# A decode layer with its backward pass on one core: the chain between the two halves reordered, side products one step later

## The chip, the cores and the metric

The kernel runs on one core of a Trainium2 chip. The metric is the device time of one execution in microseconds (us). Before the change it took 1754.85 us in the median of four runs (1751.91 to 1758.08).

## The reference, cut to what matters

```python
def _fwd_reference(A_x, A_k_cache, A_v_cache, A_wq, A_wo, B_x, B_w1, B_w3, B_w2):
    def _A_ref(x, k_cache, v_cache, wq, wo):          # B=4, H=32 heads, Sk=4096, Dh=128, D=512
        q = (x @ wq).reshape(B, Sq, H, Dh).transpose(0, 2, 1, 3)
        scores = jnp.einsum("bhqd,bhkd->bhqk", q, k_cache) * (Dh ** -0.5)
        p = _softmax(scores, axis=-1)
        o = jnp.einsum("bhqk,bhkd->bhqd", p, v_cache)
        return o.transpose(0, 2, 1, 3).reshape(B, Sq, H * Dh) @ wo
    def _B_ref(x, w1, w3, w2):                        # F=1792
        h = _silu(x @ w1) * (x @ w3)
        return h @ w2
    h = x + _A_ref(_layernorm(x), A_k_cache, A_v_cache, A_wq, A_wo)
    return h + _B_ref(_layernorm(h), B_w1, B_w3, B_w2)

_out, _vjp = jax.vjp(_f, A_x, A_k_cache, A_v_cache, A_wq, A_wo, B_w1, B_w3, B_w2)
return (_out, *_vjp(grad_out))
```

One token for each of four batch entries attends to a cache of 4096 keys and values in 32 heads, and the gradients of everything are returned. K and V are 134 MB each, and so are their gradients, so some 700 MB pass through the DMA engines.

## The kernel before, in words

The order of all instructions is written out by hand; nothing reorders them. SBUF holds 22 equal slots of about 1 MB (class `Slot`). A slot is taken from the front of the list `free` and put at its back by `give()` while the program is being written. On the chip, a load into a slot waits until the last reader or writer of the slot's former content is done. All loads are issued by one in-order queue, SP's; all large stores by GpSimd's (POOL's). So a load that waits for its slot holds up every load behind it.

**Forward half** (until about 674 us). For each of the 128 pairs of batch entry and head, K and V are loaded. `M_mm(s)` multiplies V with `PK`, the keys weighted by the probabilities, on TensorE (PE, line 436). `M_end(s)` ends that pair and gives two slots back. `kP_flush` (lines 457 to 461) turns a sum of 32 pairs round. The last pairs are 125, 126 and 127.

**The chain in the middle.** Eight loads are queued behind the last V: the two halves each of w1 and w3 (line 543), then four pages of wo of eight heads each (line 549). Transposed copies w1T and w3T are made by `w13T` (16 units, 112 transposes of 128x128 on PE at line 566; `evac_copy` at lines 216 and 218 takes each unit out of PSUM on ScalarE, ACT, or VectorE, DVE). `attn_page(pg)` multiplies the attention output with one page of wo (line 481), and DVE adds the partial sums to the residual rows `hrows` (line 487). `woT` transposes wo in place, 16 units of 8 transposes (line 575). Then come the second layernorm (`layernorm_rows`, lines 232 to 238), the transposes of its rows (line 768), the products with w1 and w3 (`gu_ps`, line 780), the element-wise work of the gate (lines 799 to 809), the products with w3T and w1T (`dn_ps`, line 817), the layernorm's gradient (lines 827 to 844), the products with the transposed wo (`dOT_ps`, line 848) and what follows from them (lines 852 to 867).

While the chain runs, w1, w3, w1T, w3T, the wo pages and eight slots of `M` fill 20 of the 22 slots. Loads of V for the backward half (`load_V2`, line 749) can use only the rest, until `gu_ps` has read w1 and w3 and `dn_ps` has read w1T and w3T.

**Backward half.** For each pair `s`, `front(s)` transposes V (`V_T`: PE line 739, ACT line 740) and forms `dP_ps` (line 1046). `back(s)` writes the gradient of V as one product on DVE (`gv`, line 1053), scales dP (lines 1068 and 1071), writes the gradient of K (`gk`, line 1053), and stores both (lines 1065 and 1075). In the loop, `front(s + 1)` precedes `back(s)`. `prefetch` lets loads of V run seven pairs ahead. After each `back(s)`, one or more steps of `side_work` are taken: a generator that forms all the other gradients in small pieces, each with one product on PE and one copy on ACT (`grad_unit`, lines 881 and 882).

Of the kernel before, what the change touches and what calls it, by code (L numbers as in the profile page):

```python
# [9 lines left out]
FP32 = mybir.dt.float32  # L10
# [14 lines left out]
def kernel(  # L25
# [448 lines left out]
    def attn_page(pg):  # L474
        last = pg == H // 8 - 1
        if pg == 0 or last:
            hold["at"] = psX.tile([P, 512], FP32, tag="x", name="at_ps")
        at_ps = hold["at"]
        for k in range(8):
            c = 0 if last else k % 4  # L480
            nc.tensor.matmul(at_ps[32 * c:32 * c + B, :], lhsT=OT_bf[:, (8 * pg + k) * B:(8 * pg + k + 1) * B],
                             rhs=wo_page(8 * pg)[:, k].rearrange("p c n -> p (c n)"),
                             start=(k == 0 if last else pg == 0 and k < 4), stop=(k == 7 if last else pg == H // 8 - 2 and k >= 4),
                             tile_position=(0, 32 * c))
        if pg >= H // 8 - 2:
            for c in range(1 if last else 4):
                nc.vector.tensor_tensor(out=hrows[:], in0=hrows[:], in1=at_ps[32 * c:32 * c + B, :], op=ALU.add)
# [90 lines left out]
    pending = deque()  # L578
    for nm, ap in (("w1", B_w1), ("w3", B_w3)):
        for i in range(2):  # L580
            pending.append((load_w13_half, nm, ap, i))
# [111 lines left out]
    weights(NGI)  # L693
    w13T(4, "sv")
    M_mm(NH - 2, 0, SJ)
    M_end(NH - 2)
    weights(NGI)
    w13T(4, "sv")
    M_mm(NH - 1, 0, SJ)
    M_end(NH - 1)  # L700
    weights(NGI)
    O_cols(NH - MC, NH)
    w13T(len(tunits), "sv")
    kP_flush(NH - 1)
    for pg in range(H // 8 - 1):
        attn_page(pg)
        woT(4, "sv")
    attn_page(H // 8 - 1)
# [43 lines left out]
    with ExitStack() as cm:  # L752
# [3 lines left out]
        psT = cm.enter_context(tc.tile_pool(name="psTm2", bufs=4, space=bass.MemoryType.PSUM))  # L756
        hs = Slot("hhat")
        hhat = hs.f(D)[0:B, :]
        while free:
            load_V2()  # L760
        layernorm_rows(hrows[:], B, hhat, rstd_h[:])
        nc.scalar.activation(out=warm[:], in_=warm[:], func=AF.Exp)
        woT(len(wo_units), "s")
        hhatT = mid.tile([P, DC, B], BF16, name="hhatT")
        hhatT_f = mid.tile([P, DC, B], FP32, name="hhatT_f")
        pt = psA.tile([P, DC, B], FP32, tag="rT", name="pt_hT")
        for c in range(DC):
            nc.tensor.transpose(pt[:, c, :], hhat[:, c * P:(c + 1) * P], ident_f[0:B, 0:B])
        nc.vector.tensor_copy(out=hhatT[:], in_=pt[:])
        nc.vector.tensor_copy(out=hhatT_f[:], in_=pt[:])  # L770
        nc.gpsimd.tensor_copy(out=hhat_bf[:], in_=hhat)
        hs.give()
        while free:
            load_V2()
        w1, w3 = mid_w["w1"], mid_w["w3"]
# [6 lines left out]
        for sl in w1 + w3:  # L782
            sl.give()
        while len(free) > 1:
            load_V2()

        rdiag = mid.tile([B, B], FP32, name="rdiag")
        nc.vector.tensor_scalar(out=rdiag[:], in0=ident_f[0:B, 0:B], scalar1=rstd_h[:], scalar2=None, op0=ALU.mult)
        rb_ps = psA.tile([P, B], FP32, tag="rT", name="rb_ps")
        nc.tensor.matmul(rb_ps[:], lhsT=ones_f[0:B, :], rhs=rdiag[:], start=True, stop=True)  # L790
        rb = mid.tile([P, B], FP32, name="rb")
        nc.vector.tensor_copy(out=rb[:], in_=rb_ps[:])
        gateT = mid.tile([P, FC, B], FP32, name="gateT")
# [15 lines left out]
        nc.vector.tensor_tensor(out=hhT_bf[:], in0=siluT[:], in1=gu_ps[:, 1], op=ALU.mult)  # L809
        V_T(0, psT)  # L810

# [8 lines left out]
        for sl in mid_w["w1T"] + mid_w["w3T"]:  # L820
            sl.give()
        while len(free) > 1:
            load_V2()
        V_T(1, psT)

# [15 lines left out]
                                       in1=u[:], op0=ALU.mult, op1=ALU.add)  # L841
        nc.vector.tensor_tensor(out=u[:], in0=u[:], in1=rb[:, None, :].to_broadcast([P, DC, B]), op=ALU.mult)
        nc.vector.tensor_tensor(out=dhT[:], in0=u[:], in1=grT[:], op=ALU.add)
# [26 lines left out]
    with ExitStack() as c2:  # L870
# [5 lines left out]
        bw3 = c2.enter_context(tc.tile_pool(name="bw3", bufs=3, reuse_waits="tile"))  # L876

        def grad_unit(dst, lhsT, rhs):
            n = rhs.shape[-1]
            ps = psg.tile([P, 512], FP32, tag="gps", name="gps")  # L880
            nc.tensor.matmul(ps[:, 0:n], lhsT=lhsT, rhs=rhs, start=True, stop=True)
            nc.scalar.copy(out=dst, in_=ps[:, 0:n])

        def side_work():
            dq_ps = psx.tile([P, 512], FP32, tag="x2", name="dq_ps")
            for s in range(NH):
                nc.tensor.matmul(dq_ps[:, s:s + 1], lhsT=M_of(s)[:, 0:Dh], rhs=dOT_f[:, s:s + 1], start=True, stop=True)
                if s % MC == MC - 1:
                    Ms[s // MC].give()
                if s % 3 == 2:  # L890
                    yield
            t = rs.f(2080)[:, 1536:1536 + NH]
            nc.vector.tensor_tensor(out=t, in0=c_rep[:], in1=kPT[:], op=ALU.mult)
# [4 lines left out]
            nc.scalar.copy(out=dqr_bf[:], in_=pt[:])  # L898
            flat = Slot("dqflat")
            for b in range(B):  # L900
                nc.sync.dma_start(out=flat.b(HD)[b:b + 1, :], in_=dqr_bf[b::B, :])
# [15 lines left out]
            for ch in range(H // HH):  # L917
# [6 lines left out]
                for hl in range(0, HH, 2):  # L924
                    pt = psg.tile([P, 2, DC, P], BF16, tag="gps", name="pt_wq")
                    for i in range(2):
                        for cc in range(DC):
                            nc.tensor.transpose(pt[:, i, cc, :], wv[:, cc, (hl + i) * Dh:(hl + i + 1) * Dh], ident_b[:])
                    nc.scalar.copy(out=wqT.b(HH * D).rearrange("p (n c) -> p n c", c=P)[:, hl * DC:(hl + 2) * DC, :],
                                   in_=pt.rearrange("p a c k -> p (a c) k"))  # L930
                    yield
                wq2.give()
                for hl in range(HH):
                    h = ch * HH + hl
                    nc.tensor.matmul(dx_ps[0:B, :], lhsT=dqT_bf[:, h * B:(h + 1) * B], rhs=wqT.b(HH * D)[:, hl * D:(hl + 1) * D],
                                     start=(h == 0), stop=(h == H - 1))
                yield
            wqT.give()
            fs = Slot("fin")
            dxhat, lnbx = fs.f(2 * D)[0:B, 0:D], fs.f(2 * D)[0:B, D:2 * D]  # L940
# [8 lines left out]
            for cc in range(DC):  # L949
                st = Slot("gwq")  # L950
                for n8 in range(HD // 512):
                    grad_unit(st.b(HD)[:, n8 * 512:(n8 + 1) * 512], xhat_bf[0:B, cc * P:(cc + 1) * P],
                              flat.b(HD)[0:B, n8 * 512:(n8 + 1) * 512])
                    yield
                nc.gpsimd.dma_start(out=out_4[cc * P:(cc + 1) * P, :], in_=st.b(HD))
                st.give()
# [5 lines left out]
            for sl in w2:  # L962
                sl.give()
            h2_bf = rs.t[0:B, 2560:2560 + D]
            nc.vector.tensor_tensor(out=h2_bf, in0=hrows[:], in1=o2_ps[0:B, :], op=ALU.add)
# [4 lines left out]
            for dst_rows, srcT in ((hh_rows, hhT_bf), (dg_rows, d_gateT_bf), (du_rows, d_upT_bf)):  # L970
                for c0 in range(0, FC, 7):
                    pt = psg.tile([B, 7, P], BF16, tag="gps", name="pt_Tr")
                    for c in range(7):
                        nc.tensor.transpose(pt[:, c, :], srcT[:, c0 + c, :], ident_b[:])
                    nc.scalar.copy(out=dst_rows[:, c0 * P:(c0 + 7) * P].rearrange("b (c f) -> b c f", f=P), in_=pt[:])
                    yield
            for i in range(2):
                st = Slot("gw2")
                for k in range(7):
                    fc = 7 * i + k  # L980
                    grad_unit(st.b(7 * D)[:, k * D:(k + 1) * D], hh_rows[:, fc * P:(fc + 1) * P], gr_bf[0:B, :])
                    yield
                nc.gpsimd.dma_start(out=out_8[i * 7 * P:(i + 1) * 7 * P, :].rearrange("(c p) j -> p c j", p=P),
                                  in_=st.b(7 * D).rearrange("p (c j) -> p c j", c=7))
                st.give()
            for (rows, out_ap) in ((dg_rows, out_6), (du_rows, out_7)):
                for i in range(2):
                    st = Slot("gw13")
                    for k in range(2):
                        for (f0_, w_) in f_chunks:  # L990
                            grad_unit(st.b(2 * F)[:, k * F + f0_:k * F + f0_ + w_],
                                      hhat_bf[0:B, (2 * i + k) * P:(2 * i + k + 1) * P], rows[:, f0_:f0_ + w_])
                            yield
                    nc.gpsimd.dma_start(out=out_ap[i * 2 * P:(i + 1) * 2 * P, :].rearrange("(c p) f -> p c f", p=P),
                                      in_=st.b(2 * F).rearrange("p (c f) -> p c f", c=2))
# [11 lines left out]
            for h0 in range(0, H, 8):  # L1007
                st = Slot("gwo")
                for k in range(8):
                    h = h0 + k  # L1010
                    grad_unit(st.b(8 * D)[:, k * D:(k + 1) * D], oflat.b(HD)[0:B, h * P:(h + 1) * P], dh_bf[0:B, :])
                    yield
                nc.gpsimd.dma_start(out=out_5[h0 * P:(h0 + 8) * P, :].rearrange("(h p) j -> p h j", p=P),
                                  in_=st.b(8 * D).rearrange("p (h j) -> p h j", h=8))
# [69 lines left out]
        for s in range(NH):  # L1084
# [5 lines left out]
            back(s)  # L1090
            step("s", 1 if s < 42 else 2 + s % 2)
        step("s", 400)
# [30 lines left out]
```

## Time and profile before

| | |
|---|---|
| median of four runs | 1754.85 us |
| profiled execution: time / span of its instructions | 1749.55 us / 1747.8 us |
| moved by DMA | 707.86 MB, mean 405 GB/s |
| busy: PE, DVE, ACT, POOL | 76%, 72%, 55%, 28% of the span |
| mean granted TensorE clock | 0.729 of full speed |

The page cuts the span into 40 slices of 43.7 us and gives the busy share of each in tenths. The view by stretches gives, for stretches that one chooses, the busy time of each engine with its count of instructions, the granted clock, the DMA share (the mean busy share of the 16 DMA engines) and what they moved. The view of waits says who waited for whom. The timeline lists instructions with the idle time ahead of them in brackets.

### The profile page before, as it was taken

The page shows a single profiled execution, that of the slowest core. Times are in us where ns is not written, and L with a number is a line of the kernel's source. Part 1 is how long each engine was busy: PE and PEld are TensorE (multiplying, and loading weights), DVE is VectorE, ACT ScalarE, POOL GpSimd, SP SyncE. Part 2 cuts the span into 40 slices and gives each one's busy share as a digit, 9 for nine tenths or more (in the row PEclk, how much of TensorE's full clock was granted, in tenths as well). Part 3 has the DMA queues.
Part 4 walks back from the last instruction along what each step waited for, and adds up shares of the span by engine and source line. Part 5 has one row for each costly group of instructions (what it writes and reads, how often), then busy time and mean ns, then how long its engine had stood idle before and what let it go on. Part 6 is the DMA issues. An engine that isn't in the chain of part 4 may idle for free.

```text
span 1747.8 us, 44078 instructions
## 1 busy us (share of the span) xinstructions
PE 1331.9 (76%) x18993; PEld 1127.6 (65%) x18993; DVE 1254.0 (72%) x1385; ACT 954.3 (55%) x1460; POOL 488.9 (28%) x805
## 2 busy tenths in 40 slices
PE   5889888788888887888877876777776778485573
PEld 4667666677666666778777875555565556365463
DVE  5899899889898995557856757566464667475585
ACT  3455445445444544555554655576666667475463
POOL 2333333333333330112421333222222223132132
PEclk8999999999999999655555556675555555556555
DMA  9999999999999998699999999999999999999997
GB/s 398 410 418 418 419 418 419 419 414 418 417 414 399 418 405 302 261 420 421 415 420 421 417 418 414 423 379 426 422 416 420 415 406 411 420 402 413 424 417 290
DMA packets 107123, 707.86 MB, mean 405 GB/s; under 512 B 11232, under 2 KB 18920, under 8 KB 23984
## 3 DMA queue, kind: packets, MB, share of 16 engines
q1 hardware_dynamic: 67280, 422.68, 59.0%
q0 software_dynamic: 39648, 282.36, 39.1%
q8 instruction: 149, 2.44, 0.5%
q14 instruction: 46, 0.38, 0.1%
HBM read 422.58 MB, written 282.34 MB: 403 GB/s over the span
## 4 chain that ended last, share of the span: by engine, by line
DMA 39%; DVE 11%; issue 6%; PE 4%; ACT 2%; POOL 1%; SPq 0%; DVEq 0%; POOLq 0%; ACTq 0%
DMA out_dram<-gk 24%; DMA out_dram<-gv 9%; DVE gk L1053 4%; DVE gv L1053 4%; DMA wq<-in_A_wq_dram 4%; ACT VT L740 1%; DMA out_dram<-gw 1%; PE pt_tps L739 1%; DMA w<-in_B_w_dram 1%; POOL P L1049 1%; DVE PK L421 1%; DMA V<-in_A_v_cache_dram 1%; PE M_ps L436 1%; DVE dS L1071 0%; DVE dSt L1068 0%
## 5 line engine op out<-in xcount | busy, mean ns | idle before, releaser
L740 ACT COPY VT<-pt_tps 128x1024 bf16<-128x1024 bf16 x512 | 492.5, 1016 | 251.2 <-PE pt_tps L739 119.3
L739 PE MATMUL pt_tps<-ident_b,V 128*128 128x128 bf16 x4096 | 464.1, 298 | 140.9 <-ACT VT L740 140.9
L739 PEld LDWEIGHTS <-V 128*128 128x128 bf16 x4096 | 413.4, 141 | 206.7 <-issue 196.9
L1053 DVE TENSOR_TENSOR gv<-P,reps 128x4096 bf16<-128x4096 bf16 x128 | 293.0, 2289 | 231.7 <-DMA out_dram<-gk 140.8
L1053 DVE TENSOR_TENSOR gk<-dS,reps 128x4096 bf16<-128x4096 bf16 x128 | 293.4, 2292 | 70.5 <-DMA out_dram<-gv 31.9
L421 DVE TENSOR_TENSOR PK<-Kn,PK 128x4096 bf16<-128x4096 bf16 x128 | 302.8, 2366 | 35.6 <-POOL PK L417 35.6
L436 PE MATMUL M_ps<-PK,Vn 128*128 128x130 bf16 x4096 | 285.9, 222 | 54.3 <-DMA Vn<-in_A_v_cache_dram 54.0
L436 PEld LDWEIGHTS <-Vn 128*128 128x128 bf16 x4096 | 252.6, 99 | 75.4 <-DMA Vn<-in_A_v_cache_dram 69.0
L328 DVE STREAM_TRANSPOSE KT<-Kn 128x512 f32<-128x512 f32 (+1 forms) x321 | 250.9, 798 | 0.5 <-issue 0.5
L323 ACT COPY KT<-pt_tps 128x1024 bf16<-128x1024 bf16 x128 | 129.4, 1012 | 192.8 <-PE pt_tps L322 154.7
L1046 PE MATMUL dP_ps<-dOT_bf,VT 128*128 128x1 bf16 x4096 | 151.8, 166 | 64.2 <-ACT VT L740 63.0
L1046 PEld LDWEIGHTS <-VT 128*128 128x128 bf16 x4096 | 142.3, 105 | 75.4 <-ACT VT L740 73.5
L1075 POOL DMA_DIRECT2D out_dram<-gk x128 | 68.2, 533 | 391.4 <-DVE gk L1053 382.2
L1065 POOL DMA_DIRECT2D out_dram<-gv x128 | 68.4, 535 | 336.2 <-DVE dSt L1068 325.0
L417 POOL COPY PK<-P_all 128x64 bf16<-128x64 bf16 x128 | 32.3, 252 | 436.8 <-ACT P_all L411 431.5
L336 POOL COPY zq<-qT_bf 128x2 bf16<-128x2 bf16 x128 | 152.1, 1189 | 0.0
L1049 POOL COPY P<-P_all 128x64 bf16<-128x64 bf16 x128 | 118.9, 929 | 0.0
L411 ACT COPY P_all<-pt_P 32x64 bf16<-32x64 bf16 x256 | 51.9, 203 | 58.0 <-PE pt_P L407 55.8
L322 PE MATMUL pt_tps<-ident_b,Kn 128*128 128x128 bf16 x1024 | 80.1, 222 | 0.7 <-DVE qrep L282 0.7
L446 PE MATMUL kP_ps<-PK,onesw 128*32 128x512 bf16 x1024 | 79.6, 388 | 0.0
L322 PEld LDWEIGHTS <-Kn 128*128 128x128 bf16 x1024 | 61.8, 99 | 26.4 <-issue 26.3
L400 ACT ACTIVATE Pn<-E,rl 128x1024 bf16<-128x1024 f32 x64 | 73.7, 1151 | 2.8 <-DVE rl L397 2.8
(221 smaller groups left out, 1292.7 us busy)
## 6 DMA issues: line engine op xcount, KB each, us to landing
Kn<-in_A_k_cache_dram SPq DMA_DIRECT2D x128, 1024.0 KB, 14.9
Vn<-in_A_v_cache_dram SPq DMA_DIRECT2D x128, 1024.0 KB, 14.9
V<-in_A_v_cache_dram SPq DMA_DIRECT2D x128, 1024.0 KB, 11.2
out_dram<-gv POOLq DMA_DIRECT2D x128, 1024.0 KB, 19.4
out_dram<-gk POOLq DMA_DIRECT2D x128, 1024.0 KB, 19.5
wq<-in_A_wq_dram SPq DMA_DIRECT2D x8, 1024.0 KB, 15.3
out_dram<-gw POOLq DMA_DIRECT2D x6, 896.0 KB, 22.1
wo<-in_A_wo_dram SPq DMA_DIRECT2D x4, 1024.0 KB, 14.5
```

The source lines that it names most:

```text
L322: nc.tensor.transpose(pt[:, i, :], Kn[:, c * GW + i, :], ident_b[:])
L323: nc.scalar.copy(out=KT[:, c * GW:(c + 1) * GW, :], in_=pt[:])
L328: nc.vector.transpose(out=KT[:, c * w_:(c + n) * w_], in_=Kn[:, c * w_:(c + n) * w_])
L336: nc.gpsimd.tensor_copy(out=zq[gi % 2][hl][:, 32:132:67], in_=qT_bf[:, s:s + 1].to_broadcast([P, 2]))
L421: nc.vector.tensor_tensor(out=PK[:, :, 0:Dh].rearrange("p j (r t) -> p j r t", t=2), in0=Ks[s].heads().rearrange("p j (r t) -> p j r t", t=2),
L436: nc.tensor.matmul(hold["M"][:], lhsT=Vn[:, j, :], rhs=PK[:, j, :], start=(j == 0), stop=(j == SJ - 1))
L446: nc.tensor.matmul(hold["kP"][32 * q:32 * (q + 1), :, :], lhsT=ones_window(w), rhs=PK[:, j0:j0 + 4, 0:Dh], start=(w == 0 and c == 0), stop ...
L739: nc.tensor.transpose(pt[:, i, :], Vn[:, g * GW + i, :], ident_b[:])
L740: nc.scalar.copy(out=VT[:, g * GW:(g + 1) * GW, :], in_=pt[:])
L1046: nc.tensor.matmul(dP_ps[:, j:j + 1], lhsT=VT[:, j, :], rhs=dOT_bf[:, s:s + 1], start=True, stop=True)
L1049: nc.gpsimd.tensor_copy(out=P2[:], in_=P_all[:, s, :, None].to_broadcast([P, SJ, 2]))
L1053: nc.vector.tensor_tensor(out=dst.rearrange("p j (r t) -> p j r t", t=2), in0=col2[:, :, None, :].to_broadcast([P, SJ, Dh // 2, 2]), in1=r ...
```

## The change

Nothing that is computed changes. The chain in the middle is written in another order, and `side_work` takes each product out of PSUM one step later:

- w3 is loaded ahead of w1. `w13T` no longer stands between the `M_mm` of the last pairs: all 16 units follow pair 127 and `kP_flush`.
- `attn_page` spreads its products over two column groups instead of four, so that two partial sums are added instead of four, and the last page has a PSUM tile of its own (`al_ps`).
- Between the pages only two units of `woT` remain. Four stand in the layernorm, five after the gate's element-wise work, five after `dn_ps`.
- The layernorm is not applied to the rows: the raw rows are transposed, and mean and inverse deviation are spread over the partitions by one small product and applied there. The slot `hhat` goes.
- `V_T(0)` and `V_T(1)` leave the chain and are made by `front(0)` and `front(1)`.
- In `side_work`, a unit's copy is issued after the next unit's product (`grad_flush`), there are more `yield`s, and one step is taken for each pair up to 43, then two, and three at every fourth pair (before: one up to 41, then two and three in turn).

```diff
@@ attn_page
-            hold["at"] = psX.tile([P, 512], FP32, tag="x", name="at_ps")
+            hold["at"] = psK.tile([P, 512], FP32, tag="kP", name="al_ps") if last else psX.tile([P, 512], FP32, tag="x", name="at_ps")
-            c = 0 if last else k % 4
+            c = 0 if last else k % 2
-            for c in range(1 if last else 4):
+            for c in range(1 if last else 2):
@@ pending
-    for nm, ap in (("w1", B_w1), ("w3", B_w3)):
+    for nm, ap in (("w3", B_w3), ("w1", B_w1)):
@@ end of the forward half
-    w13T(4, "sv")
     M_mm(NH - 2, 0, SJ)
     M_end(NH - 2)
     weights(NGI)
-    w13T(4, "sv")
     M_mm(NH - 1, 0, SJ)
     M_end(NH - 1)
     weights(NGI)
     O_cols(NH - MC, NH)
+    kP_flush(NH - 1)
     w13T(len(tunits), "sv")
-    kP_flush(NH - 1)
     for pg in range(H // 8 - 1):
         attn_page(pg)
-        woT(4, "sv")
+        if pg > 0:
+            woT(1, "s")
@@ layernorm in the middle
-        hs = Slot("hhat")
-        layernorm_rows(hrows[:], B, hhat, rstd_h[:])
+        pt = psA.tile([P, DC, B], FP32, tag="rT", name="pt_hT")
+        for c in range(DC):
+            nc.tensor.transpose(pt[:, c, :], hrows[0:B, c * P:(c + 1) * P], ident_f[0:B, 0:B])
...
+        woT(1, "s")
+        nc.scalar.sqrt(rstd_h[:], rstd_h[:])
         nc.scalar.activation(out=warm[:], in_=warm[:], func=AF.Exp)
-        woT(len(wo_units), "s")
+        woT(2, "s")
...
+        nc.tensor.matmul(rb_ps[:], lhsT=ones_f[0:B, :], rhs=rdiag[:], start=True, stop=True)
+        woT(1, "s")
...
+        nc.vector.tensor_tensor(out=hhatT_f[:], in0=pt[:], in1=rb[:, None, 0:B].to_broadcast([P, DC, B]), op=ALU.subtract)
+        nc.vector.tensor_tensor(out=hhatT[:], in0=hhatT_f[:], in1=rb[:, None, B:2 * B].to_broadcast([P, DC, B]), op=ALU.mult)
@@ gate, dn
-        V_T(0, psT)
+        woT(5, "ssvsv")
...
-        V_T(1, psT)
+        woT(len(wo_units), "s")
@@ side_work
+        def grad_flush():
+            if gu:
+                dst, ps, n = gu.pop()
+                nc.scalar.copy(out=dst, in_=ps[:, 0:n])
         def grad_unit(dst, lhsT, rhs):
...
-            nc.scalar.copy(out=dst, in_=ps[:, 0:n])
+            grad_flush()
+            gu.append((dst, ps, n))
...
             wqT.give()
+            yield
             fs = Slot("fin")
@@ backward loop
-            step("s", 1 if s < 42 else 2 + s % 2)
+            step("s", 1 if s < 44 else 2 + (s % 4 == 0))
```

## The prediction

> **What bounds the kernel now.** I read the page's slices first, then the middle in stretches of 5 us, then what SP's queue waited for, then the chain of waits.
>
> ```profile
> DMA  9999999999999998699999999999999999999997
> GB/s 398 410 418 418 419 418 419 419 414 418 417 414 399 418 405 302 261 420 421 415 420 421 417 418 414 423 379 426 422 416 420 415 406 411 420 402 413 424 417 290
> ```
>
> The DMA engines are full in all slices but the 16th, the 17th and the last, at 415 to 420 GB/s; no compute engine is. So the time is the bytes at that rate plus the time in which the DMA engines have nothing to do. The change moves no bytes in or out (three loads are queued in another order), so its worth is what it takes from that idle time.
>
> ```profile
> 685.00:690.00 5.00, 5.00 (x82) 3.94 (x79) 1.22 (x3) 2.46 (x4) 0.00 (x0) 0.98 0.69 223
> 690.00:695.00 5.00, 3.48 (x60) 3.17 (x56) 2.41 (x6) 4.25 (x5) 0.00 (x0) 1.00 0.00 1
> 695.00:700.00 5.00, 4.98 (x74) 3.98 (x75) 1.38 (x2) 2.46 (x4) 0.00 (x0) 1.00 0.56 185
> 700.00:705.00 5.00, 3.91 (x61) 3.00 (x58) 4.57 (x7) 3.50 (x4) 0.00 (x0) 1.00 0.07 28
> 705.00:710.00 5.00, 3.77 (x48) 2.66 (x46) 3.43 (x11) 1.77 (x4) 0.60 (x1) 1.00 0.00 0
> 710.00:715.00 5.00, 5.00 (x131) 4.97 (x130) 1.44 (x8) 4.26 (x6) 0.00 (x0) 0.75 0.86 292
> 715.00:720.00 5.00, 5.00 (x134) 5.00 (x133) 0.93 (x7) 3.12 (x4) 0.00 (x0) 0.50 0.99 403
> 730.00:735.00 5.00, 4.20 (x81) 3.84 (x78) 2.85 (x5) 1.73 (x3) 1.20 (x4) 0.50 0.36 149
> 735.00:740.00 5.00, 4.71 (x59) 4.41 (x58) 4.93 (x5) 3.41 (x4) 2.60 (x4) 0.50 0.91 251
> ```
>
> Columns: stretch, length, busy time of PE, PE's weight loads, DVE, ACT, POOL, granted clock, DMA share, GB/s. One minus the share, times 5 us: 1.55 + 5.0 + 2.2 + 4.65 + 5.0 + 0.7 + 0.05 + 3.2 + 0.45 = 22.8 us of idle DMA.
>
> ```profile
> SPq L749 <- PE kt_ps L460: 14.0, 1, 14.0
> SPq L749 <- PE pt_hT L768: 13.1, 1, 13.1
> 667.20 11.92 DMA w<-in_B_w_dram
> 1160.12 0.68 DVE L941 COPY fin<-dx_ps 4x512 f32<-4x512 f32 x1 [8.73 <-PE dx_ps L935]
> ```
>
> The first two lines (waits of SP's queue) say why: the two loads of V that had a slot waited 14.0 us for `kP_flush` and 13.1 us for the layernorm's rows. The third (chain of waits) is PE waiting for w3 to land before it may go on with pairs 126 and 127. The fourth (timeline) is a second hole, in the backward half: DVE stands 8.73 us for the last product of `dx_ps`, and stores and SP's queue stand behind it. In stretches of 2 us from 1160 the DMA share is 0.93, 0.59, 0.17, 0.73: 3.2 us idle.
>
> **Part 1: pairs 126 and 127 ahead of w13T.** Before, PE ended pair 125 at 673.4, waited for w3, and ran pair 126 at half clock in 3.33 us. Now pair 126 starts when its PK is ready (674.15), pair 127 when its own is (676.8, DVE's row at 674.47). Each is 1.87 us for `M_mm` and 0.55 for line 446 at full clock: end 679.2. Copies on ACT (0.9) and `kt_ps` (1.08): 681.2. Then 112 transposes. On PE 28 take 1.67, so 6.7; ACT, with 8 copies of 0.95, needs 7.6 beside them. I take 7.2 for PE: 688.4. All of w has landed by 679.2, when PE's old wait for w3 ended, and wo by some 690.
>
> **Part 2: the pages.** Eight products of one page took 0.53 us in four column groups and 1.90 in one; two groups are in no row, and lie between. I take the mean of rate, 0.95. Three pages, two units of `woT` (0.48 each) and the last page (1.90): 5.7, so 694.1. The first two additions on DVE (0.70 each) lie under the last page, which waits for no PSUM any more (1.09 before); one addition (0.68) gives `hrows` at 694.8. Before: 707.07. Twelve units of `woT` with it left this stretch.
>
> **Part 3: the layernorm.** Before, `hrows` to `gu_ps` took 2.81 us (707.07 to 709.88). Now the square root stands on ACT behind a copy of `woT`: transposes 0.42, unit 0.48, copy 0.95, root 0.20 make 2.05, where statistics alone would allow it at 1.05. Reciprocal, `rdiag`, product (0.52), copy, subtraction, multiplication: 0.15 + 0.21 + 0.52 + 0.16 + 0.2 + 0.2, with hand-overs 1.75. Sum 3.8; `gu_ps` starts at 698.6, 11.3 earlier. The table load (1.28) and two more copies queue behind the root and nothing on the path waits for them. The row form of the normalised input (0.54, now DVE's) and the second multiplication lie under `gu_ps` (2.96).
>
> **Part 4: woT in place of V_T.** From the end of `gu_ps` to `dn_ps` it was 4.0 us, `V_T(0)`'s 32 transposes at half clock. Now 40 transposes at 0.10 (the second `V_T`'s 32 took 3.22) make 4.0, while the gate's DVE work takes 2.9. After `dn_ps` (2.96) it was 3.22, now 4.0 and 0.2 for a PSUM buffer: one microsecond lost. The path is 701.6, 705.6, 708.5, 712.7 and, with the 5.2 from there to the end of `dOT_ps`, 717.9. ACT needs 4.8 for these five copies and ends before `dOT_ps` reaches its last heads. So `dOT_ps` ends 10.4 earlier than 728.27, and the first `gv` starts 3.9 later as before: 721.8 against 732.17.
>
> **Part 5: what the DMA engines make of it.** The loads up to wo end at about 690 with 1.55 us of holes; packed, at 688.5. Both free slots are now free by 681 (pair 127's V, `kP_flush`), so two loads of V follow at once, 2.5 us each at 418 GB/s: 693.5. Then idle until half of `gu_ps` has run (700.1) and a load has started (0.6, as after 709.85): 7.2 idle. Eight loads, four from w1 and w3 and four from w1T and w3T, last until 720.8.
>
> Then the stores must come, and here something is late: `V_T(0)` and `V_T(1)` are now ahead of `dP`. At ACT's 1.0 us for each quarter, behind the copies of line 1033, `dP(0)` is done 9.6 us after `dOT_ps`, and the first `gk` ends 12.5 after it (before: 9.0). The second `gv` takes the slot of the second V, and so waits for `V_T(1)`: 15.8. First bytes of the three stores, 6.9, 13.3 and 16.4 after `dOT_ps`: 724.8, 731.2, 734.3. Idle: 4.0 + 3.9 + 0.6 = 8.5, against 3.65 before. From then on DVE offers 2 MB and SP 1 MB for each 5.3 us, more than the engines move. Sum of the middle: 7.2 + 8.5 = 15.7 against 22.8, a gain of 7.1.
>
> **Part 6: side work.** Copies one step late take waits from ACT and PE, but neither is the bound: nothing, under full DMA engines. At the hole of 1160 the new `yield` does not part product and use: counting the generator's steps, the last `dx_ps` and DVE's copy of it both fall into pair 60, which has three steps (in the program's order the product stands behind `front(61)` and the copy behind `gk(60)`). But `front(61)` carries no `replicate`, as `front(56)` did, so the wait loses about 2.5 us; I take 2.5 of the 3.2 idle, bounds 0 and 3.9 (with 0.7 of smaller holes near 1430 and 1570). Side work now ends after pair 116, not 105, with the same bytes; POOL's queue gets the last four pages of it among later stores. Cover: the last loads of V and DVE's stores, which kept the engines full to 1730.
>
> Sum: 7.1 + 2.5 = 9.6 off 1749.55, the profiled execution's time, makes 1740. It lay 5.3 below the median of the runs; so 1745 for the median.
>
> [...] PE is counted at half clock after `gu_ps`, because 715 to 720 shows 0.50 with PE busy 5.00 of 5.00. [...]
>
> **Rivals.** *The hole only moves.* For it: 8.5 us of my 15.7 stand at the start of the backward half, and `V_T` waits there for ACT. If the first pairs follow one another at one store in 5 us until 745, another 5 us go: 9.6 − 5 = 4.6, so 1750. *Half clock in the chain.* Had PE half speed from 681 to 695, 112 transposes cost 5.3 more, the pages 4.7, two units 1.0: 11 us, and 1756. Against it: its longest wait there is 1 us, and 690 to 710 was granted 1.00 with waits up to 1.52. *Slower: a starved tail.* With the last `gwo` pages at pairs 105 to 116, loads and stores of the last pairs wait for slots that side work holds. POOL's idle times between stores 1575 to 1613 were 6.2, 4.29, 4.86 and 10.19, usual 2.2: 16.7 us of stalls, then hidden by queued loads. If they fall where nothing is queued, −9.6 + 16.7 gives 1762. It decides if more than half of them are uncovered. Against it: after pair 116 some 29 MB remain, 70 us of DMA, while DVE needs 11 times 5.05.
>
> **How the numbers follow.** Forecast 0.68, moved hole 0.13, half clock 0.08, starved tail 0.11. About 0.3%, 5.3 us, is what a measurement can tell from no change: below 1749.6 is faster, above 1760.1 slower. The forecast is faster in nearly all of its own range (two groups 0.53 or 1.90: −1.3 or +2.9; w13T 6.7 or 8.5; start of the backward half 3.65 or 13; side work 0 or 3.9: about 1738 to 1751), the moved hole in half of it: 0.70 faster, 0.19 same, 0.11 slower. The range goes to 1757, over half clock.
>
> **What would show it.** Right: DMA idle of 14 to 18 us between 685 and 740; `dOT_ps` ending near 718; DVE's wait for `dx_ps` still there at 5 to 7 us. Wrong: half clock before 695; `hrows` after 700; a DMA share under 0.95 between 1600 and 1725.

## The result and the profile after

The changed kernel took 1748.1 us in the median of 36 runs (1741.76 to 1760.77), beside 1753.4 us for the kernel before in 58 runs (1748.44 to 1759.38). The ratio is 0.997, with a 95% interval of 0.996 to 0.9979. So it is faster by 5.3 us; the prediction had 9.6.

The profiled execution took 1754.48 us, with a span of 1752.7, and lies 6.4 us above its kernel's median. What it shows of one place can be used; its total can't.

The slices of the page after, busy tenths and GB/s of the DMA engines:

```profile
DMA  9999999999999998899999999999999999999997
GB/s 398 410 419 418 419 418 419 418 416 418 412 418 395 418 406 322 311 419 405 423 423 420 416 418 413 415 411 354 421 412 398 411 417 403 387 412 412 414 416 299
```

Slices 16 and 17 went from 302 and 261 GB/s to 322 and 311: that is the middle. Slice 28, around 1200 us, shows 354 where before it was 426: that is in the backward half, and it is a loss (before, the weak slice was the 27th, with 379). Slice 35, around 1510, went from 420 to 387.

The stretches of the middle after (length, busy time and count of PE, PE's weight loads, DVE, ACT, POOL, then granted clock, DMA share, GB/s):

```profile
685.00:690.00 5.00, 4.89 (x72) 3.70 (x71) 2.47 (x5) 4.46 (x5) 0.00 (x0) 1.00 1.09 373
690.00:695.00 5.00, 4.23 (x37) 1.80 (x33) 2.10 (x4) 2.02 (x2) 0.00 (x0) 1.00 0.66 274
695.00:700.00 5.00, 4.09 (x92) 3.71 (x93) 2.57 (x11) 3.98 (x6) 0.00 (x0) 1.00 0.02 8
700.00:705.00 5.00, 5.00 (x98) 5.00 (x95) 2.74 (x11) 3.46 (x5) 0.00 (x0) 0.53 0.78 277
705.00:710.00 5.00, 5.00 (x134) 5.00 (x132) 1.04 (x4) 1.16 (x2) 0.00 (x0) 0.50 1.00 419
720.00:725.00 5.00, 3.99 (x34) 3.44 (x33) 2.52 (x2) 3.23 (x5) 1.12 (x4) 0.50 0.38 156
725.00:730.00 5.00, 4.27 (x63) 3.95 (x62) 1.95 (x3) 3.48 (x5) 0.47 (x1) 0.50 0.53 211
730.00:735.00 5.00, 4.32 (x70) 4.00 (x69) 4.11 (x5) 3.17 (x4) 3.37 (x3) 0.84 0.51 211
735.00:740.00 5.00, 4.06 (x55) 3.82 (x54) 4.83 (x5) 3.33 (x4) 2.54 (x3) 0.50 0.92 372
```

One minus the share, times 5 us: 1.7 + 4.9 + 1.1 make 7.7 in the first hole (690 to 705), and 3.1 + 2.35 + 2.45 + 0.4 make 8.3 in the second (720 to 740). Together 16.0, where before it was 22.8. The second hole has grown, from 3.65 to 8.3, and the first has shrunk from 19.1 to 7.7. From 740 to 745 the share is 0.99 again.

The timeline of PE and of DVE in the same execution, some lines of it (start, length, engine, line, what it does; in brackets idle time ahead of it and who ended it):

```profile
674.52 2.03 PE L436 MATMUL M_ps<-PK,Vn 128*128 128x130 bf16 x32 [0.81 <-DVE PK L421]
681.34 7.14 PE L566 MATMUL pt_w<-ident_b,w 128*128 128x128 bf16 x112
688.41 1.89 PE L481 MATMUL at_ps<-wo,OT_bf 128*4 128x512 bf16 x16
694.22 0.68 DVE L487 TENSOR_TENSOR xr<-xr,al_ps 4x512 f32<-4x512 f32 x1 [0.98 <-PE al_ps L481]
698.65 3.04 PE L792 MATMUL gu_ps<-hhatT,w 128*128 128x4 bf16 x112
705.77 0.56 PE L822 MATMUL dn_ps<-d_upT_bf,w3T 128*128 128x4 bf16 x14
714.93 3.40 PE L853 MATMUL dOT_ps<-dhT,wo 128*128 128x4 bf16 x128 [1.33 <-DVE dhT L848]
722.25 2.29 DVE L1076 TENSOR_TENSOR gv<-P,reps 128x4096 bf16<-128x4096 bf16 x1 [2.02 <-POOL P L1072]
727.92 0.25 DVE L1091 TENSOR_SCALAR dSt<-dP_ps,c_rep 128x32 f32<-128x32 f32 x1 [3.38 <-PE dP_ps L1069]
728.52 2.29 DVE L1076 TENSOR_TENSOR gk<-dS,reps 128x4096 bf16<-128x4096 bf16 x1
731.57 2.29 DVE L1076 TENSOR_TENSOR gv<-P,reps 128x4096 bf16<-128x4096 bf16 x1 [0.76 <-PE pt_tps L738]
```

Each station of the chain is some 10 to 12 us earlier: `hrows` complete at 694.9 (before 707.07), `gu_ps` at 698.65 (709.88), the end of `dOT_ps` at 718.33 (728.27), the first `gv` at 722.25 (732.17). The brackets of DVE's last lines show what the second hole waits for: the first `gk` stands 3.38 us for `dP(0)`, which comes behind `V_T(0)`, and the second `gv` another 0.76 until `V_T(1)` has read its slot.

In the backward half the product and the copy of `dx_ps` no longer wait for each other, and yet there is a hole. Stretches of 5 us, and DVE's timeline, after:

```profile
1190.00:1195.00 5.00, 0.00 (x0) 0.00 (x0) 3.91 (x5) 0.00 (x0) 0.78 (x2) 0.68 0.68 283
1195.00:1200.00 5.00, 0.84 (x8) 0.84 (x8) 4.86 (x10) 1.91 (x2) 0.00 (x0) 0.50 0.78 289
...
1520.00:1525.00 5.00, 4.04 (x61) 3.64 (x60) 4.76 (x4) 4.55 (x6) 2.49 (x2) 0.71 0.62 254
```

```profile
1191.02 2.29 DVE L1076 TENSOR_TENSOR gk<-dS,reps 128x4096 bf16<-128x4096 bf16 x1 [2.30 <-DMA out_dram<-gk]
1193.23 0.67 DVE L959 COPY fin<-dx_ps 4x512 f32<-4x512 f32 x1
...
1197.51 2.27 DVE L1076 TENSOR_TENSOR gv<-P,reps 128x4096 bf16<-128x4096 bf16 x1
```

The copy (line 959) has no bracket: the product was done at 1188. But from it to the next `gv`, DVE works 4.3 us on the small rows of the layernorm's gradient, and in that time nothing is made that could be stored. SP, whose next transfer is the row output made of these rows, issues no load from 1160.9 to 1197.6. The hole of 1160 before had these same rows behind the wait of 8.73.

### The profile page after: what moved, and what is told of

Read it like the earlier page. It is cut to its first block, busy times and chain, and to the rows that moved or that the text cites. A ratio compares the mean times of both kernels' runs of the same rounds, so it can differ in the third digit from the quotient of the medians.

```text
span 1752.7 us, 44059 instructions
## 1 busy us (share of the span) xinstructions
PE 1324.4 (76%) x18993; PEld 1121.7 (64%) x18993; DVE 1250.8 (71%) x1381; ACT 958.7 (55%) x1464; POOL 486.6 (28%) x804
## 4 chain that ended last, share of the span: by engine, by line
DMA 39%; DVE 11%; PE 5%; issue 4%; ACT 3%; POOL 1%; DVEq 0%; POOLq 0%; ACTq 0%
DMA out_dram<-gk 29%; DMA out_dram<-gv 10%; DVE gv L1076 5%; DVE gk L1076 4%; ACT VT L739 2%; PE pt_tps L738 1%; DVE PK L421 1%; PE pt_wo L575 1%; DVE dS L1094 1%; POOL P L1072 0%; PE M_ps L436 0%; DVE dSt L1091 0%; PE dP_ps L1069 0%; ACT Pn L400 0%; PE pt_w L566 0%
## 5 line engine op out<-in xcount | busy, mean ns | idle before, releaser
L738 PE MATMUL pt_tps<-ident_b,V 128*128 128x128 bf16 x4096 | 458.7, 296 | 173.0 <-ACT VT L739 167.6
L738 PEld LDWEIGHTS <-V 128*128 128x128 bf16 x4096 | 407.8, 139 | 242.0 <-issue 227.2
L336 POOL COPY zq<-qT_bf 128x2 bf16<-128x2 bf16 x128 | 152.3, 1190 | 0.0
## 6 DMA issues: line engine op xcount, KB each, us to landing
V<-in_A_v_cache_dram SPq DMA_DIRECT2D x128, 1024.0 KB, 11.6
```

Source lines behind the costliest of these rows:

```text
L336: nc.gpsimd.tensor_copy(out=zq[gi % 2][hl][:, 32:132:67], in_=qT_bf[:, s:s + 1].to_broadcast([P, 2]))
L738: nc.tensor.transpose(pt[:, i, :], Vn[:, g * GW + i, :], ident_b[:])
```

## The experiments

The kernels ran in three groups, each on another chip, and each ratio is to the kernel before on the same chip, whose medians were 1751.87, 1751.22 and 1752.29 us. Idle times of the DMA engines below are sums of one minus the share over stretches of 2 us (a share over 1 counts as 1), of one execution each; such an execution can lie several us off its kernel's median.

**The middle alone.** The changed middle, with `side_work` and the step line as before:

```diff
-            grad_flush()
-            gu.append((dst, ps, n))
+            nc.scalar.copy(out=dst, in_=ps[:, 0:n])
...
-            step("s", 1 if s < 44 else 2 + (s % 4 == 0))
+            step("s", 1 if s < 42 else 2 + s % 2)
```

> The changed middle chain with the old side work and its old steps. If the middle is worth what its DMA holes say (22.8 us before, 16.1 us in the profile of the changed kernel) and the side work costs about 2 us, this kernel is 6.5 to 7 us faster than before, 1746.5, ratio 0.996. If the forecast's side work (2.5 us gained) holds and the middle is worth less, it is 2.5 to 3 us faster, 1750.5, ratio 0.9985. If the side work does nothing, 5.3 us faster like the whole change.

Measured: 1743.93 us in 12 runs, ratio 0.9954 (0.9939 to 0.9968): 7.9 us faster than before (by the interval, 5.6 to 10.7), and by the medians faster than the whole change, though the two intervals touch (0.996 to 0.9968). Three stretches of its middle:

```profile
695.00:700.00 5.00, 4.09 (x100) 3.71 (x99) 2.33 (x11) 4.21 (x6) 0.00 (x0) 0.98 0.03 10
700.00:705.00 5.00, 5.00 (x90) 5.00 (x88) 2.75 (x11) 3.29 (x6) 0.00 (x0) 0.50 0.81 279
...
725.00:730.00 5.00, 3.81 (x64) 3.52 (x64) 3.72 (x4) 3.93 (x5) 1.31 (x2) 0.71 0.29 113
```

The same two holes stand at the same places; between 660 and 760 the idle time is 13.7 us (after 16.6, before 23.2).

**The side work alone.** The old middle with the new `side_work` and steps:

```diff
+    w13T(4, "sv")
     M_mm(NH - 2, 0, SJ)
...
-        woT(1, "s")
+        layernorm_rows(hrows[:], B, hhat, rstd_h[:])
```

> The old middle chain with the new side work and its new steps. If the side work costs: 1 to 3 us slower than before, 1755.5, ratio 1.001. By the forecast: 2.5 us faster, 1751, ratio 0.9986. The DMA hole at DVE's copy of dx_ps should be gone or shorter, and if the side work costs, new holes lie elsewhere after 1000 us.

Measured: 1754.83 us in 12 runs, ratio 1.002 (1.0003 to 1.0037): 3.0 us slower than before (by the interval, 0.5 to 6.5). The two parts add up: −7.9 and +3.0 make −4.9, and the whole change measured −5.3. So the middle gives what was forecast, and the side work costs, where 2.5 us of gain were forecast.

**Is it SP's queue?** SP issues the loads of V and, among them, four small transfers that wait for their rows. In the page's waits of SP after, two of them wait longer than before (30.8 and 11.3 before; in microseconds, times, longest):

```profile
SPq L963 <- DVE reps L962: 36.2, 1, 36.2
...
SPq L986 <- DVE reps L985: 20.4, 1, 20.4
```

In two kernels these transfers were issued by GpSimd: the changed one and, as a control, the one before.

```diff
-            nc.sync.dma_start(out=o1_2, in_=dx_bf)
+            nc.gpsimd.dma_start(out=o1_2, in_=dx_bf)
...
-                nc.sync.dma_start(out=oflat.b(HD)[b:b + 1, :], in_=O_sb[b::B, :])
+                nc.gpsimd.dma_start(out=oflat.b(HD)[b:b + 1, :], in_=O_sb[b::B, :])
```

> The changed kernel with the four small transfers of the side work (both row outputs, the two row-to-flat copies) issued by GpSimd instead of SP. SP's queue waited 36.2, 20.4 and 27.5 us for their data in the changed kernel. If the loads of V held up behind them cost DMA time (holes of 2.5 us near 1195, 1.2 near 1325, 2.6 near 1515), this is 4 to 7 us faster than the changed kernel, about 1742. If stores cover those waits, no difference, 1748.

> The kernel before with the same four small transfers issued by GpSimd. Its SP waits were 30.8, 11.3 and 25.3 us, its holes 3.2 us at 1165 and 0.7 us elsewhere. If the held-up loads cost: 3 to 4 us faster than before, 1750. If not: no difference, since DVE's wait for dx_ps, which delays the stores, is still there.

Measured: 1755.7 us (1.0022, 1.001 to 1.0034) and 1752.28 us (0.9998, 0.9986 to 1.0011), 12 runs each. On the kernel before no difference can be told. The changed one, with a ratio of 0.997 without the move, loses about 0.5% by it, some 9 us; neither of the two cases that were expected has that. Yet the hole of 1190 to 1200 is gone from its profile, though DVE works the same small rows there from 1190.16 to 1194.43:

```profile
1190.00:1192.00 2.00, 0.00 (x0) 0.00 (x0) 1.93 (x5) 0.18 (x1) 0.53 (x1) 1.00 1.03 360
1192.00:1194.00 2.00, 0.81 (x11) 0.68 (x11) 1.89 (x7) 2.00 (x3) 0.00 (x0) 0.88 0.99 340
1194.00:1196.00 2.00, 1.51 (x35) 1.43 (x34) 2.00 (x2) 1.68 (x2) 1.21 (x2) 0.50 1.01 283
```

SP had issued a load of V at 1189.32. So the small rows alone do not make that hole; SP's standing belongs to it. But another hole opens, 4.1 us from 1292 to 1302, and the time is longer. As the move puts the same transfers into the queue of the stores, it does not show what SP's waits cost by themselves. Their length does not follow the times: the kernel with two steps at every pair, below, waits 28.3 and 20.8 us at the same two places and still has a ratio of 0.9956.

**The late copies or the steps?** Two kernels part the side work's two halves. The changed kernel with the old step line, and the middle alone with the new one:

```diff
-            step("s", 1 if s < 44 else 2 + (s % 4 == 0))
+            step("s", 1 if s < 42 else 2 + s % 2)
```

> The changed kernel with the old steps (one up to pair 41, then two and three in turn); copies one step late and the added yields stay. If the new steps, which let the side work end at pair 116, are what costs the side work's 3 us: like the old side work, 1744, ratio 0.9955. If the late copies and yields cost: like the changed kernel, 1747 to 1748, ratio 0.997 to 0.998.

```diff
-            step("s", 1 if s < 42 else 2 + s % 2)
+            step("s", 1 if s < 44 else 2 + (s % 4 == 0))
```

> The changed middle, the old side work with its copies at once, and the new steps. The mirror of the run before: ratio 0.997 to 0.998 if the new steps cost, 0.9955 if the late copies and yields cost.

Measured: 1745.1 us in 6 runs, 0.9954 (0.9939 to 0.997), and 1746.41 us in 11 runs, 0.9969 (0.9957 to 0.9982). The late copies without the new steps cost nothing that can be measured: the ratio is that of the middle alone. The new steps without the late copies stand 0.0015 above it, as the whole change does, but the intervals overlap. So the step line probably carries the loss; this is not certain.

**Is it the wait for `dx_ps`?** The middle alone, with two empty steps between product and copy, and two more behind `o2`:

```diff
             wqT.give()
+            yield
+            yield
             fs = Slot("fin")
```

> The changed middle, the old steps and the old side work, and two yields each between the last product of dx_ps and DVE's copy of it, and between o2_ps and its use, so that product and use fall into different pairs. If DVE's wait for the product (8.7 us before) makes the DMA hole near 1155: hole of 2 to 3 us gone, 1742, ratio 0.994. If SP's queue, which stands some 30 us behind the row output, makes it: DVE's wait gone, the hole still there, ratio 0.9955 as without the yields.

The view of the tile `dx_ps`, what kept its reader waiting (microseconds, times), in the middle alone:

```profile
  PE dx_ps L940: 10.0, 1
```

and in the parted one:

```profile
  PE dx_ps L940: 0.5, 1
```

So the wait is gone. The stretches, in the middle alone and then in the parted one:

```profile
1150.00:1155.00 5.00, 3.69 (x59) 2.68 (x57) 4.22 (x11) 4.16 (x5) 0.00 (x0) 0.97 0.83 349
1155.00:1160.00 5.00, 2.29 (x31) 1.73 (x32) 4.85 (x4) 2.70 (x5) 0.53 (x1) 0.72 0.70 228
```

```profile
1150.00:1155.00 5.00, 4.25 (x31) 2.02 (x30) 4.37 (x8) 1.71 (x2) 0.00 (x0) 0.76 0.99 418
1155.00:1160.00 5.00, 2.94 (x57) 2.46 (x57) 1.95 (x3) 2.64 (x4) 0.79 (x2) 0.93 1.01 424
...
1240.00:1245.00 5.00, 4.10 (x53) 3.10 (x53) 0.64 (x1) 3.76 (x6) 0.00 (x0) 0.50 0.71 297
1245.00:1250.00 5.00, 2.61 (x23) 2.28 (x22) 4.93 (x5) 1.60 (x4) 0.83 (x2) 0.50 0.46 190
```

The hole of 1150 to 1160 has gone with it, 2.35 us. In its place others stand, at 1240 to 1250 (4.15 us) and later. Measured: 1746.57 us in 12 runs, 0.9971 (0.9956 to 0.9987); the profile is of the slowest of them, with 1755.85. Removing the wait won nothing. But the added steps also shift all side work behind them against the pairs, so this run alone does not price the wait.

**How long the side work lasts, and how its steps fall on the pairs.** Three more step lines on the middle alone. With the old line it ends at pair 105; with these at 120, 104 and 94:

```diff
-            step("s", 1 if s < 42 else 2 + s % 2)
+            step("s", 1 if s < 42 else 2)
```

> The changed middle, the old side work, and after pair 41 two steps for every pair: the side work ends at pair 120 (old steps 105, new steps 112 with the old side work). If the stretch of the side work costs: more than the new steps did, ratio 0.9975 or more against 0.9954 with the old steps. If only chance alignments of product and use cost: anywhere between 0.9954 and 0.997.

```diff
+            step("s", 1 if s < 42 else 2 + (s + 1) % 2)
```

> The changed middle, the old side work, three and two steps in turn instead of two and three: the side work ends at pair 104, nearly where the old one does, but the last product of dx_ps and DVE's copy of it fall into pairs 54 and 55. If the stretch is what costs: 0.9954 as with the old steps. If parting product and use costs (it stood at 0.9971 with two yields each): 0.997.

```diff
+            step("s", 1 if s < 42 else 3)
```

> The changed middle, the old side work, and three steps for every pair after 41: the side work ends at pair 94. If the stretch costs: at or below the old steps, 0.9945 to 0.9954. If a denser side work costs (its stores and copies crowd the pairs): above 0.9955.

Measured: 1744.57 us in 5 runs (0.9956, 0.9943 to 0.9969), 1749.99 in 12 (0.9984, 0.9973 to 0.9995), 1744.46 in 5 (0.9954, 0.9941 to 0.9967). The longest side work is as fast as the shortest: the stretch to pair 116 is not the cost, and no starved tail stands behind it. But taking three steps at the even pairs rather than the odd ones, nothing else, costs some 5 us beside the other two, and the intervals lie apart. The profile does not show why: it is of the fastest of the twelve runs, with 1742.52. With the shifted steps, product and copy of `dx_ps` fall into pairs 54 and 55; with three steps at every pair they are parted too, and that kernel is fast. So it isn't the parting either.

**Where the transposes of wo stand.** The middle alone with `woT` back between the pages, as before:

```diff
-        if pg > 0:
-            woT(1, "s")
+        woT(4, "sv")
```

> The changed middle with the old side work and old steps, but the transposes of wo put back: twelve units between the pages and four in the layernorm, none after the gate and none after dn_ps. By the working of the prediction the first hole of the DMA engines grows by some 4 us (hrows near 699.5), the chain's end moves by only -1 to -2 us (about 716.5), the second hole shrinks by as much as the first grew, and the time is that of the kernel with them spread, 0.9946 to 0.9954. If the start of the loads is what counts, it loses the 4 us: 0.9975.

```profile
700.00:705.00 5.00, 4.32 (x125) 4.13 (x123) 1.95 (x10) 4.57 (x7) 0.00 (x0) 0.90 0.02 3
...
720.00:725.00 5.00, 4.25 (x51) 4.02 (x51) 2.29 (x1) 3.83 (x6) 1.56 (x4) 0.55 1.01 419
725.00:730.00 5.00, 3.78 (x66) 3.45 (x63) 2.77 (x3) 3.90 (x6) 0.35 (x1) 0.79 0.68 279
730.00:735.00 5.00, 4.21 (x54) 3.96 (x52) 4.86 (x4) 2.33 (x4) 2.92 (x3) 0.50 0.79 326
```

`gu_ps` starts at 702.6 instead of 698.4 in the middle alone, and the first hole is 4 us longer. But the work is then out of the way behind the gate and `dn_ps`: `dOT_ps` ends at 716.9, only 1.0 later than in the middle alone. The loads that start later also last longer: 720 to 725 is full, and the second hole is 1.6 + 1.05 = 2.65 us up to 735, against 5.55 in the middle alone. The sum from 660 to 760 is 15.5, against 13.7. Measured: 1744.15 us in 6 runs, 0.9955 (0.994 to 0.997): not to be told apart from the middle alone. The spread of `woT` over three gaps moves idle time from the first hole to the second, and is worth nothing by itself that can be measured.

**The start of the backward half.** The middle alone, with both of the first `gv` products written ahead of the wait for `dP(0)`, where DVE stood 3.36 us:

```diff
+            if s == 0:
+                pairs(1)
+                back_v(0)
+                back_v(1)
             dP_ps = bwd.pop(s)
```

> The changed middle, the old side work, and at the start of the backward half the first two gv written one after the other, ahead of the wait for dP of pair 0, the second no longer in the slot that V_T of pair 1 frees. By the working of the prediction the hole there falls from 8.5 to 6.1 us: 2 us faster than without, 1742, ratio 0.9942. If the hole is set by V_T on ACT and PE alone, the stores only change places and it is 0.9955.

```profile
720.00:725.00 5.00, 3.99 (x37) 3.60 (x36) 3.44 (x2) 3.73 (x6) 1.58 (x4) 0.50 0.49 205
725.00:730.00 5.00, 3.54 (x67) 3.20 (x66) 3.71 (x4) 4.09 (x5) 0.79 (x2) 0.84 0.95 383
730.00:735.00 5.00, 4.51 (x61) 4.43 (x59) 2.66 (x4) 2.20 (x3) 0.77 (x2) 0.50 0.60 249
735.00:740.00 5.00, 4.27 (x57) 3.96 (x55) 3.50 (x5) 3.19 (x4) 2.53 (x3) 0.50 0.74 234
```

The store now fills 725 to 730 (0.95 against 0.53 after and 0.29 in the middle alone). The idle time comes back at 730 to 740, where 2.0 + 1.3 us are lost: there DVE waits 2.08 us for `dP(1)`, and the second `gk` starts only at 732.92. From 720 to 740 the sum is 6.1 us, in the middle alone 5.85. Measured: 1742.94 us in 6 runs, 0.9948 (0.993 to 0.9966): the lowest median of the study, 0.5% under the kernel before, but not to be told apart from the middle alone.

## Why the prediction was right, and where it was wrong

**The total.** The verdict, faster, stands on the middle, which won 0.8 us more than its sum; the side work missed by 5.5. By the total alone, 5.3 us lies nearer to the rival *the hole only moves* (4.6) than to the forecast (9.6): it is the profile and the run of the middle alone that tell the two apart.

**Parts 1 to 4, the chain: right, to half a microsecond, and partly by luck.** Pair 126 started at 674.5 (predicted 674.15), the last transpose ended at 688.5 (688.4), `hrows` were complete at 694.9 (694.8), `gu_ps` started at 698.65 (698.6), `dn_ps` at 705.8 (705.6), `dOT_ps` ended at 718.3 (717.9), the first `gv` started at 722.25 (721.8). The price that was in no row, a page in two column groups, was taken as 0.95; two pages took 1.89. The reason given for it does not yield it: the mean of the two rates makes 0.83, and 0.95 is half of the 1.90 of one group. The granted clock stayed at 1.00 until 700, so the rival with half clock in the chain falls. Behind that, the agreement is this execution's: nine other profiles hold the same chain, and their clock from 705 to 710 was 0.50 once, 0.77 and 0.79, and 0.84 six times; `dOT_ps` ended between 715.9 and 718.0.

**Part 5, what the DMA engines make of it: right.** 7.2 + 8.5 predicted, 7.7 + 8.3 in the profile; the middle alone, whose second hole was shorter (5.9 up to 745) at a higher clock (0.84 against 0.50 from 705 to 710), measured −7.9 where −7.1 was the sum. The late item was named correctly: `V_T` behind `dOT_ps`, seen in the 3.38 ahead of the first `gk` and the 0.76 ahead of the second `gv`. The first three stores were issued at 724.84, 731.11 and 734.16, and the prediction had 724.8, 731.2 and 734.3. The rival *the hole only moves* had 5 us more of idle time up to 745; the second hole ended by 740, and 740 to 745 has a share of 0.99. (In those 5 us only 252 GB/s were moved, which at 418 would be 2.0 us lost; the middle alone moved 415 there.)

**The clock behind `gu_ps`.** PE behind `gu_ps` was counted at half clock, by the row of 715 to 720. After shows 0.53 and 0.50 from 700 to 710 with PE busy 5.00 of 5.00, as the row had it. What lowers the clock there is not known from these runs. No long idle time of PE stands ahead of it: the longest from 681 to 700 in the profile is 0.78 us. That PE runs transposes from 701.55 to 705.77 does not explain it by itself: 112 of them ran from 681.34 to 688.48 at 1.00.

**Part 6, side work: wrong, in sign.** The step that failed is "the wait loses about 2.5 us; I take 2.5 of the 3.2 idle, bounds 0 and 3.9". Two things were wrong in it. The wait did not shrink to 5 to 7 us, it vanished in the profiled execution. And the time does not hang on it. Among the kernels with the changed middle, three have a wait of 10.0 us in their profiles (the middle alone, the early transposes of wo, the changed start) and ratios of 0.9948 to 0.9955. Of those with 0.5 or less, three (the late copies with the old steps, two steps at every pair, three at every pair) have 0.9954 to 0.9956, and three (the whole change, the new steps alone, the parted one) 0.9969 to 0.9971: without the wait none is faster. Nor does the idle time go with it: after's profile has 1.6 + 1.1 = 2.7 us around 1195, where for 4.3 us DVE makes nothing that could be stored and SP stands behind the same rows, and the first three of those without the wait have a hole of 2.3 to 4.2 us each between 1138 and 1196. The lower bound of 0 was too high as well: "Side work now ends after pair 116, not 105, with the same bytes" was taken to cost nothing, and the new schedule cost 3.0 us. The only loss that was priced there was the starved tail.

Where the 3 us go is not shown. From 760 to 1600 the DMA engines idle 12.4 us after and 8.3 before, but after's profile is of an execution 6.4 us above its median, and such sums do not follow the times: the side work alone idles 8.8 there, the changed start, one of the fastest, 11.6, and the shifted steps 6.0. From 1450 to 1600 the three kernels with the whole new side work idle 3.0 to 3.5 us and nine others 0.6 to 1.6; yet the parted one has 3.0, and the kernel before with its transfers moved to GpSimd, which is not slower, has 3.3. **What stays open** is how the phase of the steps against the pairs costs time. The length of the side work and DVE's wait for `dx_ps` are not the cause; SP's queue has a part in the hole of 1195, and what its waits cost is not known.

"Copies one step late take waits from ACT and PE, but neither is the bound: nothing" held: with the old steps the late copies cost and gain nothing that can be measured. The starved tail, the slower rival, did not come: after's DMA engines idle 1.4 us from 1600 to 1740.

## What to carry to other kernels

In a kernel that its DMA engines bound, count a change by the DMA idle time that it removes (here the middle's idle time went from 22.8 to 16.0 us, and the middle alone was 7.9 us faster): follow the chain to the first store and the first load that it releases, and don't credit transposes that only change place (0.9955 with those of wo between the pages, 0.9954 with them spread). Work that is interleaved with a stream by a step count is a change of its own, though it moves no byte: here one shift of its phase cost 5 us, as much as the whole change won, so measure it apart from the rest. And before a wait is counted as a loss, look at what runs behind it and at what each queue waits for: when it ends earlier, the same hole may open for the next reason (here the wait for `dx_ps` went from 10.0 us to 0.5, and the ratio from 0.9954 to 0.9971).

## What the hardware showed that was not expected

- **One instruction stream, two clocks.** From 705 to 710, with PE busy 5.00 of 5.00 in both, the granted clock was 0.50 after and 0.84 in the middle alone, whose instructions there are the same; the first `gv` started at 722.25 and 719.84. With three steps at every pair, again the same instructions there, it was 0.50.
- **Full engines, fewer bytes.** In the backward half there are stretches in which the DMA share is 0.99 to 1.0 and yet the rate is far under the usual 418 GB/s: 740 to 745 after moved 252 GB/s at a share of 0.99, and 1395 to 1400 moved 315, also at 0.99. Over the stretches from 760 to 1740 with a share of 0.97 or more the mean was 419.2 GB/s before, 416.0 after, 417.8 in the middle alone, each in one execution. Over a thousand microseconds, 0.4% of rate is 4 us, as much as the idle times that were being compared; what sets it is not known from these runs.
- **One move, two prices.** Four small transfers moved from SP's queue to GpSimd's cost some 9 us in one kernel (1.0022 against 0.997) and nothing that can be measured in the other (0.9998). Why is not known.
